# Attention scores and transposes issued on two 64-row halves of the array, and the first MLP's `w_in` low words joined on VectorE

## The chip, the cores and the metric

The kernel runs on one core of a Trainium2 chip. The metric is device microseconds of one execution, as a median of several runs. Five engines work side by side, each in the order in which its own instructions were written: PE (TensorE: PE for the matmuls, PEld for the loading of the stationary operand), DVE (VectorE), ACT (ScalarE), POOL (GpSimd) and SP (SyncE, which issues the DMAs). They wait for each other by semaphores.

## The reference, cut to what matters

Three layers follow each other. Attention runs over 8 batches of 576 tokens with 8 heads of 64, its keys and values averaged over groups of 8 tokens (72 remain):

```python
k_p = k.reshape(B, H, Sp, pool, D).mean(axis=3)          # Sp = 72
scores = scale * np.matmul(q, k_p.transpose(0, 1, 3, 2))
attn = np.exp(scores - scores.max(-1)); attn /= attn.sum(-1) + 1e-09
out = np.matmul(attn, v_p)
```

Then a rational MLP, with tokens 4608, model 512, hidden 2048: `h = x @ w_in; g = P(h) / (Q(h) + 1e-6); y = g @ w_out`, with P a cubic and Q built of |h| and h². Then a gated MLP with hidden 1536: `(sigmoid(y @ w_gate) * (y @ w_val)) @ w_out2`. The weights of both MLPs arrive as float64.

## The kernel before, in words

**Layout.** The 4608 tokens are 36 tiles of 128 tokens; four tiles are a block of 512. The first MLP goes block by block, 16 hidden slices of 128 each: 144 steps, each with `g1` (12 matmuls of 512 columns into a bank `h`, then a chain on ACT and DVE, then `g` with its low part on POOL) and `g2` (12 matmuls into four banks `acc`). Every large product is made of three fp32r matmuls of high and low parts (`mm3`, lines 628 to 630).

**Attention** of a tile (`tile_attention`, from line 544) is spread between these steps:

- *Scores*, line 569, tile `sc`. The pooled keys `kp` of a batch, two heads above each other on the 128 partitions, are copied by ACT into a block-diagonal tile `kbd` (`place_keys`, line 476), with zeros elsewhere. A matmul over all 128 rows then gives two heads at once: stationary 128x128 (queries), moving 128x144 (`kbd`). Four of them give the eight heads, two in each of two PSUM banks. An fp32 matmul appears as two records in the trace, each with its own load, so a tile has 8.
- *Softmax*: maximum and subtraction on DVE, Exp on ACT, sum and reciprocal on DVE, scaling on POOL (line 586).
- *Transposes*, line 594, tile `pta`: eight, each with stationary 128x72 (a head of `e`) and the 128x128 identity moving; a transpose is one record. ACT copies the two banks to `aT` (line 596).
- *Product with the values*, line 610, tile `psx`: the two heads of a pair go to the upper and lower 64 columns of the array, with stationary 72x64 (`vh`).

A tile that spans two batches does its scores once for each, so 36 tiles have 40 score groups.

**Weights of the first MLP.** `conv1` turns a float64 slice in `stage` (high and low 32-bit words interleaved) into fp32 bits: ACT rescales the high words (line 296), ACT scales the low words (298), DVE shifts the high words (299, an int32 TENSOR_SCALAR), POOL adds the two (303). `conv2` splits the result into a high part (ACT, line 308) and a low part (line 310): by DVE for `w_in`, by POOL for `w_out`. The first eight slices of `w_in` and of `w_out` are converted apart (512 wide), the other eight in pairs (1024 wide). `background` converts the second MLP's weights in the same way.

**Order.** A planner places every task by a table of costs, ranks and free buffers, and the engines' instructions are written in that order, so a new cost or buffer moves instructions all through the program. In the planner, tasks with `port=True` on DVE are not started while POOL is busy, nor POOL's while such a task runs. Attention's banks come from the four banks of `h` (from block 1 on at most three at a time).

Of the kernel before, what the change touches and what calls it, by code (L numbers as in the profile page):

```python
# [12 lines left out]
U32 = mybir.dt.uint32  # L13
AF = mybir.ActivationFunctionType
ALU = mybir.AluOpType
AX = mybir.AxisListType
# [172 lines left out]
def attention_moe_glu_kernel(ctx: ExitStack, tc: tile.TileContext, q, k, v, w_in, w_out, ca, cb, w_gate, w_val, w_out2, out):  # L189
    nc = tc.nc  # L190

    B, H, S, D = v.shape
# [40 lines left out]
    slots = {"W": [f"w{i}" for i in range(NF1 + FS + NR)], "ST": [f"st{i}" for i in range(6)],  # L233
             "h": [f"b{i}" for i in range(4)], "su": [f"su{i}" for i in range(3)], "y": [f"y{i}" for i in range(3)],
             "m": [f"m{i}" for i in range(3)], "g": [f"g{i}" for i in range(3)], "xs": ["xs0", "xs1"],
             "raw": [f"raw{i}" for i in range(3)], "e": ["e"], "aT": ["aT"], "kp": ["kp"], "vp": ["vp"],
             "vh": ["vh0", "vh1"], "kbd": ["kbd"]}
# [50 lines left out]

    def conv1(raw, rank):
        n = raw.size * 4 * P
        r = [(raw, ("in", x)) for x in range(raw.size)]
        def hw(): return raw.t[:, :, 1]
        def lw(): return raw.t[:, :, 0]
        plan("ACT", act(n), rank, lambda: nc.scalar.activation(hw().bitcast(F32), hw().bitcast(F32), AF.Prelu, scale=2.0 ** -112, alpha=2.0 ** 32),  # L296
             w=[(raw, 1)], r=r)
        plan("ACT", act(n), rank, lambda: nc.scalar.activation(lw(), lw().bitcast(U32), AF.Copy, scale=2.0 ** -29), w=[(raw, 0)], r=r)
        plan("DVE", 0.07 + n * 0.00065, rank, lambda: nc.vector.tensor_scalar(out=hw(), in0=hw(), scalar1=3, scalar2=None, op0=ALU.logical_shift_left),
             w=[(raw, 1)], port=True)  # L300
        for x in range(raw.size):
# [47 lines left out]
    def weights(f, rank, load_i, load_o, rank_o):  # L349
        if f < 8:  # L350
            for make, put, r, rl in ((wi_load, wi_parts, rank, load_i), (wo_load, wo_parts, rank_o, load_o)):
                raw = raw_buf(f"raw{f}", "cv")
                make(f, raw, rl)
                conv1(raw, r)
                put(f, raw, r)
            return
        raw = raw_buf(f"raw{f}", "cv" if f < SEG else "cv2", 2)
        wi_load(f, raw, load_i, 0)
        wo_load(f, raw, load_o, 1)
        conv1(raw, rank)  # L360
        wi_parts(f, raw, rank, 0)
        wo_parts(f, raw, rank_o, 1)

# [89 lines left out]
    kbd = small([P, NJ, 2, SP], "kbd", ["kbd"])  # L453
    vh, xs, rawq, turned, pooled = {}, {}, {}, [], {}

    def k_cols(c):
# [2 lines left out]
    def keys(b, rank, rank_load):  # L459
# [10 lines left out]
    def place_keys(b, rank):  # L470
        kp = pooled.pop(b)
        for js, cs in ((slice(0, NJ // 2), (0, 1, 2)), (slice(NJ // 2, NJ), (2, 3, 4))):
            for e in range(2):
                half = slice(e * D, (e + 1) * D)
                def fn(e=e, js=js, half=half):
                    nc.scalar.activation(kbd.t[half, js, e], kp.t.rearrange("p (j s) -> p j s", s=SP)[half, js], AF.Copy)
                plan("ACT", act(SP * 2), rank, fn,
                    w=[(kbd, (js.start, e))], r=[(kp, c) for c in cs])

    def values0(rank, rank_load):  # L480
        vp = small([P, NCH, D], "vp", ["vp"])
# [68 lines left out]
    def tile_attention(i, rank, gate_on=[]):  # L550
# [8 lines left out]

        for x, (b, n) in enumerate(parts):  # L560
            rows = slice(x * n, (x + 1) * n)
            if i == first[b]:
                place_keys(b, rank)
            for g in range(2):
                sc = psum("sc", own, kind)

                def fn(g=g, sc=sc):
                    for j in (2 * g, 2 * g + 1):
                        nc.tensor.matmul(sc.t[:, (j % 2) * 2 * SP:(j % 2 + 1) * 2 * SP], raw.t[:, j * P:(j + 1) * P], kbd.t[:, j].rearrange("p e s -> p (e s)"), start=True, stop=True)  # L569
                plan("PE", 0.5, rank, fn, w=[sc], r=[raw, (kbd, (2 * g, 0)), (kbd, (2 * g, 1))],  # L570
                     after=(turned[-1:] if blk > 1 else turned[-3:-2]) + gate_on)
                hs = slice(4 * g, 4 * g + 4)
                scv = lambda sc=sc, rows=rows: sc.t[rows, :4 * SP].rearrange("p (h s) -> p h s", s=SP)
                plan("DVE", dve(288) - 0.04, rank, lambda hs=hs, scv=scv, rows=rows: nc.vector.reduce_max(mx.t[rows, hs], scv(), axis=AX.X), w=[(mx, (g, x))], r=[sc])
                plan("DVE", dve(288) - 0.04, rank, lambda hs=hs, scv=scv, rows=rows, n=n: nc.vector.tensor_tensor(
                    out=e_.t[rows, hs, :SP], in0=scv(), in1=mx.t[rows, hs].unsqueeze(2).to_broadcast([n, 4, SP]), op=ALU.subtract),
                    w=[(e_, (g, x))], r=[sc, (mx, (g, x))])
# [4 lines left out]
        def fn():  # L582
# [3 lines left out]
        plan("POOL", 1.12, rank, lambda: nc.gpsimd.tensor_tensor(  # L586
            out=e_.t[:, :, :SP], in0=e_.t[:, :, :SP], in1=r.t.unsqueeze(2).to_broadcast([P, H, SP]), op=ALU.mult), w=[e_], r=[r])
        aT = small([P, H, P], "aT", tmp_where(blk, "aT") + (["ST"] if blk >= 2 else []), "tmp" if blk < 2 else None)
        for g in range(2):
            pta = psum("pta", own, kind)  # L590

            def fn(g=g, pta=pta):
                for h in range(4 * g, 4 * g + 4):
                    nc.tensor.transpose(pta.t.rearrange("p (h t) -> p h t", t=P)[:SP, h % 4], e_.t[:, h, :SP], ident)  # L594
            pt = plan("PE", 0.44, rank, fn, w=[pta], r=[e_])
            plan("ACT", act(512) - 0.08, rank, lambda g=g, pta=pta: nc.scalar.activation(  # L596
                aT.t[:SP, 4 * g:4 * g + 4], pta.t.rearrange("p (h t) -> p h t", t=P)[:SP], AF.Copy), w=[(aT, g)], r=[pta])
        turned.append(pt)
        waiting.append((i, parts, aT))
        if blk >= 2 and i % 2 == 0:  # L600
# [128 lines left out]

    T0 = -20.0  # L730
    values_at = {}
    for c in range(1):
        plan("DVE", 0.6, T0, lambda: nc.vector.memset(kbd.t, 0.0), w=[kbd])
# [57 lines left out]
    for n in range(N1):  # L791
# [6 lines left out]
        x = n - last_step  # L798
        if x == BX:
            bar = plan("-", 0.0, n, "late", after=[t for t in plan.tasks if any(b.where and b.where[0] in  # L800
                       ("ST", "raw", "e", "aT", "kp", "vp", "vh", "kbd", "mx0", "mx1", "r0", "r1") for b in t.bufs)])
# [28 lines left out]
    with tc.manual_schedule():  # L830
# [7 lines left out]
        pools.update(w=wp, b=ps, su=rot, y=rot, m=rot, g=g_p, xs=xs_p, raw=raw_p, e=ap1, aT=ap1, kp=ap1, vp=ap1, vh=ap1, kbd=ap1,  # L838
                     mx=sm, r=sm)
        for t in jobs:  # L840
            if t.fn == "late":
# [358 lines left out]
```

## Time and profile before

| | us |
|---|---|
| Median of 3 runs (lowest, highest) | 1736.67 (1735.71, 1737.2) |
| The profiled execution's own time | 1734.64 |
| Its span, first to last instruction | 1732.6 |
| PE busy in the span | 1709.0 (99%) |
| PEld busy | 1553.5 (90%) |
| DVE busy | 1235.0 (71%) |
| ACT busy | 1046.6 (60%) |
| POOL busy | 730.0 (42%) |

A matmul's record is longer than its share of the engine: matmuls overlap, and what each adds is seen from the distance of the starts. A burst's cost is therefore read from the start of a matmul to the start of a later one. The trace gives starts in hundredths of a microsecond.

### The profile page before, as it was taken

What the parts mean: (1) busy time and instruction counts of PE and PEld (TensorE: products, weight loads), DVE (VectorE), ACT (ScalarE), POOL (GpSimd) and SP (SyncE); (2) the same over time, 40 slices, a digit from 0 to 9 for tenths busy, and PEclk for the clock granted to TensorE, in tenths of its full rate; (3) what the DMA queues carried; (4) which work ended last, traced back from release to release, by engine and by line L of the source; (5) the groups of instructions that cost most, each with busy time, mean ns of one, the idle gap of its engine ahead of it and who ended that gap; (6) DMA issues with size and microseconds to landing.
All of it is one profiled execution on the core that took longest, in us unless ns stands there. A gap on an engine that the chain in (4) does not pass through costs nothing.

```text
span 1732.6 us, 28635 instructions
## 1 busy us (share of the span) xinstructions
PE 1709.0 (99%) x10044; PEld 1553.5 (90%) x10044; DVE 1235.0 (71%) x2146; ACT 1046.6 (60%) x1957; POOL 730.0 (42%) x807
## 2 busy tenths in 40 slices
PE   7899999999999999999999999999999999999999
PEld 6688888888888888788889999999999999999999
DVE  7898888888887878788786466466466467457456
ACT  6999778787877878898885244244244234235234
POOL 6675356454644646777544320330330330330320
PEclk9999999999999999999999999999999999999999
DMA  7675463545535446775753998888888888888856
GB/s 242 190 278 197 158 192 127 177 145 181 187 116 184 146 157 187 227 239 185 235 181 120 301 317 279 277 265 279 272 272 280 277 265 279 272 270 279 255 181 207
DMA packets 180867, 384.61 MB, mean 222 GB/s; under 512 B 24692, under 2 KB 92276, under 8 KB 180724
## 3 DMA queue, kind: packets, MB, share of 16 engines
q1 hardware_dynamic: 180724, 382.78, 67.4%
q8 instruction: 80, 1.31, 0.3%
q14 instruction: 63, 0.52, 0.1%
HBM read 322.96 MB, written 58.72 MB: 220 GB/s over the span
## 4 chain that ended last, share of the span: by engine, by line
PE 93%; ACT 2%; DMA 1%; DVE 1%; POOL 1%; issue 0%; SPq 0%; POOLq 0%; ACTq 0%
PE h L628 17%; PE h L630 17%; PE h L629 17%; PE acc L628 7%; PE acc L630 7%; PE acc L629 7%; PE acc L1044 5%; PE acc L1043 5%; PE acc L1042 5%; PE sc L569 2%; PE psx L610 2%; PE pta L594 2%; DMA stage<-in_moe_w_in_dram 0%; ACT stage L296 0%; DMA rawv<-in_v_dram 0%
## 5 line engine op out<-in xcount | busy, mean ns | idle before, releaser
L933 DVE TENSOR_TENSOR t<-h,t 128x384 f32<-128x384 f32 x360 | 200.8, 558 | 251.2 <-PE h L630 123.0
L668 POOL TENSOR_TENSOR g<-y,g 128x512 fp32r<-128x512 f32 x143 | 186.6, 1305 | 205.3 <-ACT g L666 175.7
L1002 POOL TENSOR_TENSOR ga<-t 128x384 f32<-128x384 f32 x48 | 48.9, 1019 | 452.5 <-DVE t L933 445.6
L628 PE MATMUL h<-xs,wi 128*128 128x512 f32 x576 | 228.9, 397 | 5.7 <-ACT aT L596 3.6
L628 PE MATMUL acc<-g,wo 128*128 128x512 f32 x576 | 230.1, 399 | 0.0
L630 PE MATMUL acc<-g,wo 128*128 128x512 f32 x576 | 225.2, 391 | 1.9 <-POOL g L668 1.9
L630 PE MATMUL h<-xs,wi 128*128 128x512 f32 x576 | 225.3, 391 | 0.0
L629 PE MATMUL h<-xs,wi 128*128 128x512 f32 x576 | 225.2, 391 | 0.0
L629 PE MATMUL acc<-g,wo 128*128 128x512 f32 x576 | 224.6, 390 | 0.0
L1044 PE MATMUL acc<-wo,go 128*128 128x256 f32 x756 | 213.9, 283 | 0.0
L1043 PE MATMUL acc<-wo,go 128*128 128x256 f32 x756 | 213.9, 283 | 0.0
L1042 PE MATMUL acc<-wo,go 128*128 128x256 f32 x756 | 213.9, 283 | 0.0
L628 PE MATMUL h<-xS,wq 128*128 128x384 f32 x576 | 192.4, 334 | 0.0
L630 PE MATMUL h<-xS,wq 128*128 128x384 f32 x576 | 192.4, 334 | 0.0
L629 PE MATMUL h<-xS,wq 128*128 128x384 f32 x576 | 192.4, 334 | 0.0
L947 ACT ACTIVATE t<-h 128x384 f32<-128x384 f32 x72 | 35.3, 491 | 242.2 <-PE h L630 238.4
L662 DVE SCALAR_TENSOR_TENSOR y<-y,coef,h 128x512 f32<-128x512 f32 x144 | 107.2, 744 | 70.9 <-ACT h L661 70.5
L1044 PEld LDWEIGHTS acc<-wo,go 128*128 128x128 f32 x756 | 145.1, 192 | 0.0
L1043 PEld LDWEIGHTS acc<-wo,go 128*128 128x128 f32 x756 | 145.1, 192 | 0.0
L1042 PEld LDWEIGHTS acc<-wo,go 128*128 128x128 f32 x756 | 145.1, 192 | 0.0
L628 PE MATMUL h<-xA,wq 128*128 128x384 f32 x432 | 144.3, 334 | 0.0
L629 PE MATMUL h<-xA,wq 128*128 128x384 f32 x432 | 144.3, 334 | 0.0
(129 smaller groups left out, 4258.1 us busy)
## 6 DMA issues: line engine op xcount, KB each, us to landing
wq<-w2d SPq DMA_DIRECT2D x252, 512.0 KB
wo<-wo2d SPq DMA_DIRECT2D x126, 512.0 KB
wo<-wod SPq DMA_DIRECT2D x96, 512.0 KB
w2d<-stage SPq DMA_DIRECT2D x36, 512.0 KB
wo2d<-stage SPq DMA_DIRECT2D x84, 128.0 KB
rawk<-in_k_dram SPq DMA_DIRECT2D x32, 256.0 KB
rawq<-in_q_dram SPq DMA_DIRECT2D x32, 256.0 KB
rawv<-in_v_dram SPq DMA_DIRECT2D x32, 256.0 KB
```

The lines of the kernel that those rows point to most:

```text
L569: nc.tensor.matmul(sc.t[:, (j % 2) * 2 * SP:(j % 2 + 1) * 2 * SP], raw.t[:, j * P:(j + 1) * P], kbd.t[:, j].rearrange("p e s -> p (e s)"), ...
L628: nc.tensor.matmul(out_, wl, xh, start=start, stop=False, skip_group_check=on)
L629: nc.tensor.matmul(out_, wh, xh, start=False, stop=False, skip_group_check=on)
L630: nc.tensor.matmul(out_, wh, xl, start=False, stop=stop, skip_group_check=on)
L662: plan("DVE", 0.66, rank, lambda: STT(out=y.t, in0=y.t, scalar=coef[:, 0:1], in1=h.t, op0=ALU.add, op1=ALU.mult), w=[y], r=[h])
L668: plan(on, cost, rank, lambda: eng.tensor_tensor(out=g.t[:, 1], in0=y.t, in1=g.t[:, 0].bitcast(F32), op=ALU.subtract), w=[(g, 1)], r=[y, ( ...
L933: nc.vector.tensor_tensor(out=out_, in0=a, in1=b, op=ALU.add)
L947: nc.scalar.activation(t["u"], b[1], AF.Copy)
L1002: eng.tensor_tensor(out=dst, in0=x, in1=y, op=ALU.mult)
L1042: nc.tensor.matmul(a, gh, wh, start=s_ == 0 and not on, stop=False, skip_group_check=on)
L1043: nc.tensor.matmul(a, gh, wl, start=False, stop=False, skip_group_check=on)
L1044: nc.tensor.matmul(a, gl, wh, start=False, stop=s_ == NS - 1, skip_group_check=on)
```

## The change

Scores: the tile `kbd` and its copies go. The matmuls read `kp` directly, 16 records of stationary 64x128 and moving 64x72, with the heads of the upper 64 rows (`g` = 0) and of the lower 64 rows (`g` = 1) in turn, each half of the rows into a bank of its own. Both banks belong to one task. `kp` has two buffers. Transposes: 16 instead of 8, each of 64 rows (tokens) with the 64x64 part of the identity moving, the halves in turn, each half into its own bank; ACT's two copies to `aT` now take a half of the tokens each. Weights: for every `w_in` slice, and for both of the slices converted in pairs, the low words' ACT instruction and POOL's add are replaced by one DVE SCALAR_TENSOR_TENSOR (shift right by 29, then or); the low part of `w_in` goes from DVE to POOL.

```diff
-    def conv1(raw, rank):
+    def conv1(raw, rank, fused=False):
...
-        plan("ACT", act(n), rank, lambda: nc.scalar.activation(lw(), lw().bitcast(U32), AF.Copy, scale=2.0 ** -29), w=[(raw, 0)], r=r)
+        if not fused:
+            plan("ACT", act(n), rank, lambda: nc.scalar.activation(lw(), lw().bitcast(U32), AF.Copy, scale=2.0 ** -29), w=[(raw, 0)], r=r)
...
+            if fused:
+                plan("DVE", 0.75, rank, lambda o=o: nc.vector.scalar_tensor_tensor(out=hw()[:, o], in0=lw()[:, o], scalar=29, in1=hw()[:, o],
+                     op0=ALU.logical_shift_right, op1=ALU.bitwise_or), w=[(raw, ("t", x))], r=r + [(raw, 1)], port=True)
+                continue
...
-        conv2(raw, wi[f], rank, 0, x)
+        conv2(raw, wi[f], rank, 1, x)
...
-                conv1(raw, r)
+                conv1(raw, r, make is wi_load)
...
-        conv1(raw, rank)
+        conv1(raw, rank, True)
...
+            sc = [psum("sc", own, kind) for _ in range(2)]
+
+            def fn(b=b, sc=sc):
+                for j in range(NJ):
+                    for g in range(2):
+                        nc.tensor.matmul(sc[g].t[:, j * SP:(j + 1) * SP], raw.t[g * D:(g + 1) * D, j * P:(j + 1) * P],
+                                         pooled[b].t[g * D:(g + 1) * D, j * SP:(j + 1) * SP], start=True, stop=True)
+            plan("PE", 0.6, rank, fn, w=sc, r=[raw, pooled[b]],
...
-                    for j in (2 * g, 2 * g + 1):
-                        nc.tensor.matmul(sc.t[:, (j % 2) * 2 * SP:(j % 2 + 1) * 2 * SP], raw.t[:, j * P:(j + 1) * P], kbd.t[:, j].rearrange("p e s -> p (e s)"), start=True, stop=True)
-                plan("PE", 0.5, rank, fn, w=[sc], r=[raw, (kbd, (2 * g, 0)), (kbd, (2 * g, 1))],
...
+        pta = [psum("pta", own, kind) for _ in range(2)]
+
+        def fn(pta=pta):
+            for h in range(H):
+                for g in range(2):
+                    rows = slice(g * D, (g + 1) * D)
+                    nc.tensor.transpose(pta[g].t.rearrange("p (h t) -> p h t", t=D)[:SP, h], e_.t[rows, h, :SP], ident[rows, rows])
+        pt = plan("PE", 0.55, rank, fn, w=pta, r=[e_])
...
-                    nc.tensor.transpose(pta.t.rearrange("p (h t) -> p h t", t=P)[:SP, h % 4], e_.t[:, h, :SP], ident)
-            pt = plan("PE", 0.44, rank, fn, w=[pta], r=[e_])
```

Three places show how instructions move. PE, in the middle of the first MLP, before: `acc` and `h` are the big products, the sixth row a tile's transposes, and the scores of the next tile stand one product later.

```order
L628 MATMUL acc_2139<-g,wo_1976 128x512
L629 MATMUL acc_2139<-g,wo_1976 128x512
L630 MATMUL acc_2139<-g,wo_1976 128x512
L594 MATMUL pta<-ident,e 72x128 x8
L628 MATMUL acc_2146<-g,wo_1976 128x512
L629 MATMUL acc_2146<-g,wo_1976 128x512
L630 MATMUL acc_2146<-g,wo_1976 128x512
L569 MATMUL sc<-kbd,rawq 128x144 x4
L628 MATMUL h<-xs,wi_1523 128x512
```

PE at the same kind of place now:

```order
L625 MATMUL acc_2228<-g,wo_2048 128x512
L626 MATMUL acc_2228<-g,wo_2048 128x512
L627 MATMUL acc_2228<-g,wo_2048 128x512
L590 MATMUL pta<-ident,e 72x64 x16
L625 MATMUL acc_2219<-g,wo_2048 128x512
L626 MATMUL acc_2219<-g,wo_2048 128x512
L627 MATMUL acc_2219<-g,wo_2048 128x512
```

The burst still stands alone between two full-array products; its instructions are twice as many and half as high. Over the program 36 score and 33 transpose bursts stand so.

ACT at the start of the program before, where `wi` and `wo` are the high parts (line 308) of the weights, `stage` the words (296, 298) and `kbd` the copies of the keys:

```order
L308 ACTIVATE wi_448<-stage 128x512
L296 ACTIVATE stage<-stage 128x512
L619 ACTIVATE xs<-psx 128x4x128
L298 ACTIVATE stage<-stage 128x512
L476 ACTIVATE kbd<-kp 64x2x72 x4
L296 ACTIVATE stage<-stage 128x512
L298 ACTIVATE stage<-stage 128x512
L654 ACTIVATE u<-h,coef 128x512
```

The same place now:

```order
L616 ACTIVATE xs<-psx 128x4x128
L314 ACTIVATE wi_492<-stage 128x512
L297 ACTIVATE stage<-stage 128x512
L300 ACTIVATE stage<-stage 128x512
L297 ACTIVATE stage<-stage 128x512
L651 ACTIVATE u<-h,coef 128x512
```

The four copies and one of two low-word instructions (298, now 300) are gone from ACT's row.

DVE at the start of the program before, around the low parts (310) of the first two `w_in` slices:

```order
L620 SCALAR_TENSOR_TENSOR xs<-psx,xs 128x4x128 x2
L310 TENSOR_TENSOR wi_372<-stage,wi_372 128x512
L299 TENSOR_SCALAR stage<-stage 128x512 x2
L620 SCALAR_TENSOR_TENSOR xs<-psx,xs 128x4x128
L310 TENSOR_TENSOR wi_448<-stage,wi_448 128x512
```

The same place now:

```order
L617 SCALAR_TENSOR_TENSOR xs<-psx,xs 128x4x128 x2
L306 SCALAR_TENSOR_TENSOR stage<-stage 128x512
L617 SCALAR_TENSOR_TENSOR xs<-psx,xs 128x4x128
L301 TENSOR_SCALAR stage<-stage 128x512 x2
L306 SCALAR_TENSOR_TENSOR stage<-stage 128x512
```

On DVE the joining instruction (306) has taken the place of the low part (310), one for one.

## Rows read from the trace of the kernel before

**Rows 1.** Windows: length; PE, PEld, DVE, ACT, POOL busy (records); clock; DMA.
```profile
30.00:57.00 27.00, 21.13 (x134) 17.30 (x132) 23.04 (x43) 22.19 (x42) 18.23 (x21) 0.87 0.65 209
57.00:107.40 50.40, 45.75 (x243) 36.55 (x243) 47.10 (x75) 49.23 (x86) 40.14 (x41) 1.00 0.64 211
107.40:130.00 22.60, 22.60 (x100) 18.71 (x101) 20.09 (x30) 22.52 (x37) 14.75 (x14) 1.00 0.83 277
130.00:845.00 715.00, 712.45 (x3721) 592.26 (x3720) 588.48 (x976) 578.92 (x1042) 405.89 (x483) 1.00 0.53 175
```

**Rows 2.** Windows of tile sc alone, from 107.4: PE, PEld, DVE busy (records).
```profile
107.40:845.00 737.60, 35.88 (x248) 34.83 (x248) 53.69 (x124) 1.00 0.54 178
```

**Rows 3.** Windows of tile pta alone: PE, PEld, ACT busy (records).
```profile
107.40:845.00 737.60, 29.45 (x224) 24.59 (x224) 30.31 (x56) 1.00 0.54 178
```

**Rows 4.** PE timeline, one score burst: start, length, line, shapes, records.
```profile
443.56 1.14 PE L569 MATMUL sc<-kbd,rawq 128*128 128x144 f32 x8
...
444.78 0.40 PE L629 MATMUL h<-xs,wi 128*128 128x512 f32 x1
```

**Rows 5.** PE timeline, one transpose burst.
```profile
453.44 1.03 PE L594 MATMUL pta<-ident,e 128*72 128x128 f32 x8
...
454.54 0.40 PE L629 MATMUL acc<-g,wo 128*128 128x512 f32 x1
```

**Rows 6.** PE timeline, a burst on the array's column halves.
```profile
412.63 0.40 PE L630 MATMUL acc<-g,wo 128*128 128x512 f32 x1
412.96 1.09 PE L610 MATMUL psx<-aT,vh 72*64 72x128 f32 x16
413.89 1.04 PE L610 MATMUL psx<-stage,vh 72*64 72x128 f32 x16
414.86 0.50 PE L628 MATMUL acc<-g,wo 128*128 128x512 f32 x1
415.19 0.39 PE L629 MATMUL acc<-g,wo 128*128 128x512 f32 x1
```

**Rows 7.** PE timeline, another such burst, its second part 64 columns wide.
```profile
277.35 1.10 PE L610 MATMUL psx<-stage,vh 72*64 72x64 f32 x32
278.38 0.50 PE L628 MATMUL h<-xs,wi 128*128 128x512 f32 x1
```

**Rows 8.** PEld timeline, two loads of one pair of column halves.
```profile
413.23 0.14 PEld L610 LDWEIGHTS psx<-aT,vh 72*64 72x64 f32 x2
```

**Rows 9.** PEld timeline, ten loads of 72 columns in a row.
```profile
20.11 0.73 PEld L511 LDWEIGHTS vps<-vp,sel 128*72 128x72 f32 x10
```

**Rows 10.** PE timeline, from 128-row to 64-row matmuls: two windows' rows.
```profile
21.14 0.69 PE L511 MATMUL vps<-vp,sel 128*72 128x64 f32 x6
...
21.49 0.34 PE L511 MATMUL vps<-vp,sel 64*72 64x64 f32 x2
```

**Rows 11.** Groups by form, PEld: shapes, records; busy us, mean ns; idle before.
```profile
L594 PEld LDWEIGHTS pta<-ident,e 128*72 128x72 f32 x288 | 31.8, 117 | 13.6 <-POOL e L586 6.1 <-ACT aT L596 1.9 <-issue 0.3
...
L511 PEld LDWEIGHTS vps<-vp,sel 128*72 128x72 f32 x22 | 1.6, 145 | 0.0
L511 PEld LDWEIGHTS vps<-vp,sel 64*72 64x72 f32 x2 | 0.2, 138 | 0.1
```

**Rows 12.** Groups of ACT from 18 to 107.4.
```profile
L298 ACT ACTIVATE stage<-stage 128x512 int32<-128x512 uint32 (+1 forms) x18 | 13.1, 733 | 0.0
...
L476 ACT ACTIVATE kbd<-kp 64x144 f32<-64x144 f32 x4 | 1.3, 322 | 0.0
```

**Rows 13.** Groups of DVE from 18 to 107.4.
```profile
L310 DVE TENSOR_TENSOR wi<-stage,wi 128x512 fp32r<-128x512 f32 x9 | 8.0, 892 | 0.7 <-ACT wi L308 0.7
...
L663 DVE SCALAR_TENSOR_TENSOR h<-u,h 128x512 f32<-128x512 f32 x9 | 6.2, 684 | 0.0
```

**Rows 14.** Groups of POOL from 18 to 107.4.
```profile
L303 POOL TENSOR_TENSOR stage<-stage 128x512 int32<-128x512 int32 x20 | 21.3, 1078 | 11.2 <-DVE stage L299 4.0 <-issue 2.7 <-ACT h L661 2.1
...
L310 POOL TENSOR_TENSOR wo<-stage,wo 128x512 fp32r<-128x512 f32 x8 | 10.5, 1315 | 0.7 <-ACT wo L308 0.6
```

More of the change, by code (lines that the diff above doesn't have):

```diff
@@ L235, in attention_moe_glu_kernel @@
              "m": [f"m{i}" for i in range(3)], "g": [f"g{i}" for i in range(3)], "xs": ["xs0", "xs1"],
-             "raw": [f"raw{i}" for i in range(3)], "e": ["e"], "aT": ["aT"], "kp": ["kp"], "vp": ["vp"],
-             "vh": ["vh0", "vh1"], "kbd": ["kbd"]}
+             "raw": [f"raw{i}" for i in range(3)], "e": ["e"], "aT": ["aT"], "kp": ["kp0", "kp1"], "vp": ["vp"],
+             "vh": ["vh0", "vh1"]}
     slots.update({f"acc{e}": [f"b{4 + e}"] for e in range(NJ)})
@@ L451, in small @@
         return Buf(name, shape, F32, where, kind)
-    kbd = small([P, NJ, 2, SP], "kbd", ["kbd"])
     vh, xs, rawq, turned, pooled = {}, {}, {}, [], {}
@@ L468, in keys @@
         pooled[b] = kp
[L470 to L478, printed above, removed]
     def values0(rank, rank_load):
@@ L561, in tile_attention @@
             rows = slice(x * n, (x + 1) * n)
-            if i == first[b]:
-                place_keys(b, rank)
-            for g in range(2):
-                sc = psum("sc", own, kind)
-                def fn(g=g, sc=sc):
-                    for j in (2 * g, 2 * g + 1):
-                        nc.tensor.matmul(sc.t[:, (j % 2) * 2 * SP:(j % 2 + 1) * 2 * SP], raw.t[:, j * P:(j + 1) * P], kbd.t[:, j].rearrange("p e s -> p (e s)"), start=True, stop=True)
-                plan("PE", 0.5, rank, fn, w=[sc], r=[raw, (kbd, (2 * g, 0)), (kbd, (2 * g, 1))],
[L571 to L574, printed above, removed]
+            sc = [psum("sc", own, kind) for _ in range(2)]
[5 more added lines that the diff above has]
+            plan("PE", 0.6, rank, fn, w=sc, r=[raw, pooled[b]],
+                 after=(turned[-1:] if blk > 1 else turned[-3:-2]) + gate_on)
+            for g in range(2):
+                hs = slice(g, H, 2)
+                scv = lambda sc=sc[g], rows=rows: sc.t[rows, :4 * SP].rearrange("p (h s) -> p h s", s=SP)
+                plan("DVE", dve(288) - 0.04, rank, lambda hs=hs, scv=scv, rows=rows: nc.vector.reduce_max(mx.t[rows, hs], scv(), axis=AX.X), w=[(mx, (g, x))], r=[sc[g]])
                 plan("DVE", dve(288) - 0.04, rank, lambda hs=hs, scv=scv, rows=rows, n=n: nc.vector.tensor_tensor(
                     out=e_.t[rows, hs, :SP], in0=scv(), in1=mx.t[rows, hs].unsqueeze(2).to_broadcast([n, 4, SP]), op=ALU.subtract),
-                    w=[(e_, (g, x))], r=[sc, (mx, (g, x))])
+                    w=[(e_, (g, x))], r=[sc[g], (mx, (g, x))])
         plan("ACT", act(576), rank, lambda: nc.scalar.activation(e_.t[:, :, :SP], e_.t[:, :, :SP], AF.Exp, scale=scale / POOL),
@@ L588, in tile_attention @@
         aT = small([P, H, P], "aT", tmp_where(blk, "aT") + (["ST"] if blk >= 2 else []), "tmp" if blk < 2 else None)
-        for g in range(2):
-            pta = psum("pta", own, kind)
-            def fn(g=g, pta=pta):
-                for h in range(4 * g, 4 * g + 4):
-                    nc.tensor.transpose(pta.t.rearrange("p (h t) -> p h t", t=P)[:SP, h % 4], e_.t[:, h, :SP], ident)
-            pt = plan("PE", 0.44, rank, fn, w=[pta], r=[e_])
+        pta = [psum("pta", own, kind) for _ in range(2)]
[5 more added lines that the diff above has]
+        pt = plan("PE", 0.55, rank, fn, w=pta, r=[e_])
+        for g in range(2):
             plan("ACT", act(512) - 0.08, rank, lambda g=g, pta=pta: nc.scalar.activation(
-                aT.t[:SP, 4 * g:4 * g + 4], pta.t.rearrange("p (h t) -> p h t", t=P)[:SP], AF.Copy), w=[(aT, g)], r=[pta])
+                aT.t[:SP, :, g * D:(g + 1) * D], pta[g].t.rearrange("p (h t) -> p h t", t=D)[:SP], AF.Copy), w=[(aT, g)], r=[pta[g]])
         turned.append(pt)
@@ L731, in attention_moe_glu_kernel @@
     values_at = {}
-    for c in range(1):
-        plan("DVE", 0.6, T0, lambda: nc.vector.memset(kbd.t, 0.0), w=[kbd])
     warm = psum("warm", ["acc2"])
@@ L800, in attention_moe_glu_kernel @@
             bar = plan("-", 0.0, n, "late", after=[t for t in plan.tasks if any(b.where and b.where[0] in
-                       ("ST", "raw", "e", "aT", "kp", "vp", "vh", "kbd", "mx0", "mx1", "r0", "r1") for b in t.bufs)])
+                       ("ST", "raw", "e", "aT", "kp", "vp", "vh", "mx0", "mx1", "r0", "r1") for b in t.bufs)])
             rawx[0] = Buf("rawx", [P, 8 * TB], F32, ["xs"])
@@ L837, in attention_moe_glu_kernel @@
         stage_t.append(stage.tile([P, len(slots["ST"]) * 8 * P], F32, name="stage"))
-        pools.update(w=wp, b=ps, su=rot, y=rot, m=rot, g=g_p, xs=xs_p, raw=raw_p, e=ap1, aT=ap1, kp=ap1, vp=ap1, vh=ap1, kbd=ap1,
+        pools.update(w=wp, b=ps, su=rot, y=rot, m=rot, g=g_p, xs=xs_p, raw=raw_p, e=ap1, aT=ap1, kp=ap1, vp=ap1, vh=ap1,
                      mx=sm, r=sm)
```

## The prediction

> **What bounds the kernel now.** I read the busy time by stage first, then single bursts in PE's timeline, then the groups of the start. The windows show two regimes. From 107.4 us to the end of attention PE is the bound: it is busy for 22.60 of 22.60 us and then for 712.45 of 715.00, at full clock [rows 1]. There a microsecond of PE is a microsecond of the kernel, and what other engines shed is worth nothing. Before 107.4 PE waits: from 30 on it is busy for 21.13 of 27.0 and 45.75 of 50.4 us, so 10.5 us are idle, and the granted clock averages 0.87 in the first of the two, some of it at the lower of two levels. In the second, ACT is busy for 49.23 of 50.4 us and DVE for 47.10 [rows 1]: two engines, almost equally full. The change has one part for each regime.
>
> **The unit.** A plain 512-column matmul costs 22.60 / 100 = 0.226 us [rows 1]; I use 0.227. A burst costs the distance from its first start to the real start of the big matmul after it. That one's start is modelled too early, so I take the second big matmul's start less 0.227. The scores cost 444.78 - 0.227 - 443.56 = 0.99 us [rows 4], 0.122 for each of the 8 records, and the transposes 454.54 - 0.227 - 453.44 = 0.87 [rows 5], 0.109 each. Behind 107.4 there are 248 / 8 = 31 score groups [rows 2] and 224 / 8 = 28 tiles' transposes [rows 3].
>
> **What halves of the array cost: read from the value product.** It already runs on halves, of the columns. Its 16 records of 128 moving columns take 0.93 us (412.96 to 413.89), which is 8 x 0.109 and a first load of 0.05: two matmuls go in the time of one [rows 6]. Their loads run side by side: two, of 137 ns each, within 0.14 us [rows 8]. So halves do overlap. But entering and leaving cost time. The last full matmul streams until 412.63 + 0.23 = 412.86, and the first half begins at 412.96: 0.10 idle, and then its load is not hidden. At the end, 414.86 - 413.89 = 0.97 is 8 x 0.109 and 0.10 idle, and the next full load (415.19 - 0.23 - 414.86 = 0.10 to 0.11) lies open [rows 6]. Whether row halves pay this too is seen once: from 128-row to 64-row matmuls at 21 us. Four full ones at 0.065 from 21.14 on stream until 21.39, and the first 64-row one comes at 21.49: the same 0.10 [rows 10].
>
> **What a pair costs.** Matmuls are half as long now: 72 moving columns instead of 144 is 0.061 us. But the score's load keeps its 128 columns. Ten loads of 72 columns stand (0.73 - 0.145) / 9 = 0.065 apart [rows 9, 11], though their matmuls of 64 columns alone would need half of the 0.109 of 128 columns. Pairs with loads of 64 columns stand (278.38 - 277.35 - 0.10) / 16 = 0.058 apart [rows 7]. That is 0.9 ns a column, so loads of 128 columns set a pace of 0.107 (the load that lies open) to 0.116 (0.9 x 128). I take 0.112. Above it the bound is 0.122, where such loads hide now [rows 4]. Below it, if a load of half the rows took half the time, it is 0.061. The trace's loads of 64 rows took 138 ns against 145 with 128 rows [rows 11], so I stay near the upper end.
> The Trainium skill (TensorE: Matmul & The Clock Gate, section LDWEIGHTS) states a load as columns over 1.2 GHz, whatever the number of rows. By that the pace would be at least 0.107 us; the trace's 138 against 145 ns agrees.
>
> **Scores, after.** 0.10 idle + 0.11 first load + 7 x 0.112 + 0.06 last matmul + 0.10 idle + 0.11 open load = 1.26, say 1.25 us, against 0.99. 31 x 0.26 = +8.1 us. What the halves save in streaming (8 x 0.122 against 8 x 0.112) is less than the two changes cost.
>
> **Transposes, after.** Eight pairs with 64 moving columns; a transpose's load of 72 columns is 28 ns shorter than a matmul's (117 against 145 [rows 11]), so the matmuls set the pace: 0.058. 0.10 + 0.03 + 8 x 0.058 + 0.10 + 0.11 = 0.80 against 0.87. 28 x -0.07 = -2.0 us.
>
> So the stage behind 107.4 gains 6.1 us. The waits that are added, two banks at once for a burst, I cost at nothing: queued behind them on PE are the big products, but before the change PE idled for only 2.55 us in the whole stage [rows 1], and a slower PE gives the others more time. If a burst once misses its bank, it is some tenths.
>
> **The start.** From 18 to 107.4 ACT has 18 low-word instructions (16 of 512, 2 of 1024; 13.1 us) and four key copies (1.3) [rows 12]. Eight and both wide ones go, by columns 60% of the 13.1 (6144 of 10240): 7.9, with the copies 9.2 us, or some 8 as such records overlap their neighbours. DVE loses nine or ten low parts of 0.892 [rows 13] and gains 8 + 2 x 2 = 12 joining instructions. No row shows such an instruction. The nearest are an SBUF pair (310, 0.892 with its port waits) and a SCALAR_TENSOR_TENSOR (0.684) [rows 13]; I take 0.75, which makes 12 x 0.75 - 9.5 x 0.892 = +0.5 us, with -0.3 and +2.2 at the ends. POOL loses 12 adds of 1.078 and gains nine or ten low parts of 1.315 [rows 14]: -0.4 us. So ACT is freed, and DVE, which has 3.3 us of idle time in 50.4 [rows 1], is late next. I take 3 us off the start. At best all of PE's idle time from 30 on (10.5 us) and what the low clock costs (0.13 x 27 = 3.5) go: -14. At worst, each early `w_in` slice is ready later, as its low part takes 1.315 on POOL instead of 0.892 and stands there in the row with values and gates: 10 x 0.42 = +4. The dearer scores of this stage, nine groups, are within that.
>
> **Sum.** +8.1 - 2.0 - 3.0 = +3.1 us. On the profiled execution's 1734.64 that is 1737.7. This execution lay 2.0 below the median of the runs, 1736.67, to which the result compares: 1739.8.
>
> **Rivals.**
> *Faster by halves.* (a) The loads of 64 rows take half the time: a pair 0.061, scores 0.86, 31 x -0.13 = -4.0; with -2.0 and -3 this is -9, 1728. Against it: 138 and 145 ns. (b) A change to row halves costs no idle time: scores 8 x 0.112 + 0.01 = 0.91, transposes 0.47: -2.5 - 11.2 - 3 = -17, 1720. Against it stand rows 6 and 10. (c) Both at once, a pair costing hardly more than one of its matmuls: scores 0.50, transposes 0.46, -15.2 - 11.5 - 3 = -30, 1707. For it speaks only that the column halves overlap so well.
> The Trainium skill (TensorE: Matmul & The Clock Gate, section Measured speedup vs the span model) gives a packed group as one matmul's time and about 4 ns for each further tile, which is (c). It holds for long streams; for bursts of 16 between full matmuls rows 6 show 0.36 us on top.
> *Slower by serial halves.* Row halves share what column halves do not, and their loads go one after another: scores 16 x 0.112 + 0.36 = 2.15, 31 x 1.16 = +36; transposes unchanged from my sum; +31, 1768. It decides as soon as two loads of a pair start more than 0.1 us apart. If the matmuls don't overlap either, transposes are 16 x 0.056 + 0.36 = 1.26 and the time 1780: then the change does not do what it says. Against it speaks the overlap in rows 6 and 8, though of columns.
> *Slower by the start.* POOL's low parts hold back the first products, and the start grows by 4 instead of shrinking by 3: 1736.67 + 6.1 + 4 = 1746.8. It decides if PE's first continuous stretch begins after 107.4. For it: POOL was busy for 40.14 of 50.4 us, and these parts are on the way to the first products. Against it: its sum of work does not grow.
>
> **How the numbers follow.** My forecast has 0.46, with a start between -6 and 0 and so 1736.8 to 1742.8, at 1739.8. Faster by halves has 0.30: (a) 0.12, (b) 0.10, (c) 0.08. Serial halves have 0.11, of which 0.04 at 1780. The longer start has 0.13. About 0.2% (3.5 us) can be told from no change here. The forecast's own band lies across that bound: 0.25 same, 0.19 slower, 0.02 faster. Of the longer start 0.02 is same and 0.11 slower. So faster is 0.30 + 0.02 = 0.32, same 0.27, slower 0.19 + 0.11 + 0.11 = 0.41. The range leaves out (c) and the serial halves, together 0.19, and takes in (b) with a little room and the longer start: 1718 to 1750.
>
> **What would show it.** In PE's timeline of the changed kernel: a score burst of 1.25 us between big matmuls, loads in pairs that start within some ns, pairs 0.11 apart; a transpose burst of 0.80, pairs 0.058 apart; 0.10 idle at either end. Pairs of scores at 0.06 say (a), no idle ends say (b), pairs at 0.2 say serial halves. For the start: PE continuously busy from some 104 us, ACT with a few us of idle time between 57 and there, DVE with almost none. I am wrong if the scores cost less than 0.9 us or more than 1.5, or if that point moves by more than 6 us either way.

## The result, and the profile after

The changed kernel takes 1747.58 us (median of 6 runs, 1746.97 to 1751.46); the kernel before took 1736.4 beside it (6 runs, 1735.13 to 1737.39). The ratio is 1.007, with an interval of 1.0057 to 1.0083: 11.2 us slower, where 3.1 had been forecast. The profiled execution took 1746.97 (1734.64 before); its span is 1745.1 against 1732.6, 12.5 longer.

Windows of the kernel after, columns as in [rows 1]:

```profile
0.00:30.00 30.00, 22.26 (x240) 20.68 (x240) 20.23 (x43) 13.72 (x26) 17.27 (x41) 0.75 0.85 272
30.00:57.00 27.00, 20.59 (x112) 16.05 (x112) 20.03 (x35) 16.93 (x30) 14.54 (x18) 0.71 0.56 181
57.00:107.40 50.40, 47.35 (x324) 37.10 (x325) 45.76 (x80) 46.16 (x81) 40.84 (x41) 1.00 0.58 179
107.40:130.00 22.60, 21.97 (x97) 17.55 (x96) 22.18 (x33) 21.42 (x37) 13.75 (x13) 1.00 0.91 321
130.00:845.00 715.00, 709.48 (x4155) 571.68 (x4154) 591.09 (x969) 560.13 (x998) 397.81 (x472) 1.00 0.53 175
```

ACT is relieved as forecast (30 to 57: 16.93 against 22.19; 57 to 107.4: 46.16 against 49.23), yet PE is idle more behind 130: 5.5 us against 2.55. And from 30 to 57 us the granted clock is 0.71 where it was 0.87.

A score burst of the kernel after, PE and then PEld (start, length, shapes, records), which answers to [rows 4]:

```profile
450.51 0.39 PE L627 MATMUL acc<-g,wo 128*128 128x512 f32 x1
450.83 1.11 PE L562 MATMUL sc<-kp,rawq 64*128 64x72 f32 x16
451.88 0.50 PE L625 MATMUL h<-xs,wi 128*128 128x512 f32 x1
452.22 0.39 PE L626 MATMUL h<-xs,wi 128*128 128x512 f32 x1
```

```profile
450.83 0.97 PEld L562 LDWEIGHTS sc<-kp,rawq 64*128 64x128 f32 x16 [0.35 <-DVE u L653]
451.88 0.19 PEld L625 LDWEIGHTS h<-xs,wi 128*128 128x128 f32 x1
```

Counted from the end of the product ahead, so that the idle time on entering is in it, the burst costs 452.22 - 0.227 - (450.51 + 0.227) = 1.25 us. (The prediction's unit, from the burst's first start, leaves that out, though its sum of 1.25 has it in.) The 16 loads of some 0.19 us each fill only 0.97 us, so two run side by side; eight pairs stand (0.97 - 0.19) / 7 = 0.111 apart. Ahead of the burst 450.83 - 450.74 = 0.09 is idle, and behind it the next full load lies open: 452.22 - 0.227 - 451.88 = 0.11.

A transpose burst of the kernel after, PE and PEld, against [rows 5]:

```profile
461.31 0.39 PE L627 MATMUL acc<-g,wo 128*128 128x512 f32 x1
461.63 0.64 PE L590 MATMUL pta<-ident,e 64*72 64x64 f32 x16
462.20 0.50 PE L625 MATMUL acc<-g,wo 128*128 128x512 f32 x1
462.53 0.39 PE L626 MATMUL acc<-g,wo 128*128 128x512 f32 x1
```

```profile
461.62 0.48 PEld L590 LDWEIGHTS pta<-ident,e 64*72 64x72 f32 x16 [0.35 <-issue]
```

It costs 462.53 - 0.227 - (461.31 + 0.227) = 0.77 us. Over all bursts behind 107.4, counted in this way, the medians are 1.249 us for the scores (0.994 before) and 0.773 for the transposes (0.882 before).

**An account.** The first MLP has 3456 matmuls of 512 columns (six groups of 576). I cut the span at the start of the 301st and of the last: what lies ahead is the start, what lies between is the stretch, which holds 3155 such matmuls, the 31 score groups, the transposes of 28 tiles and all value products of that part, in every kernel below; the granted clock in it is 1.00 on both sides. Before, the 301st starts at 126.12, after at 128.55:

```profile
126.12 0.39 PE L628 MATMUL h<-xs,wi 128*128 128x512 f32 x1
```

```profile
128.55 0.39 PE L625 MATMUL acc<-g,wo 128*128 128x512 f32 x1
```

The start is 2.4 longer. The stretch grew from 813.84 to 823.93, by 10.1: the bursts' share is 31 x 0.255 - 28 x 0.109 = +4.85, so 5.2 us are something else. What follows is the same (792.6). PE's waits from 107.4 to 860 in the kernel after (in total, times, longest):

```profile
PE h L625 <- DVE y L661: 2.1, 2, 1.1
PE h L625 <- DVE e L570: 2.0, 2, 1.4
PE acc L627 <- POOL g L665: 1.5, 2, 0.9
PE sc L562 <- DVE xs L617: 0.2, 1, 0.2
```

Most are an `h` product that waits until DVE has done with a bank (2.1 us for the last reader of an earlier `h`, line 661; 2.0 for the scores' subtraction, line 570). PE's gaps in the stretch sum to 6.2 us in ten places, against 2.55 in three before. Between two big products a wait costs more than its gap shows, because the record of the product ahead is longer than its share and the first load behind the gap lies open:

```profile
571.21 0.39 PE L627 MATMUL acc<-g,wo 128*128 128x512 f32 x1
572.67 0.50 PE L625 MATMUL h<-xs,wi 128*128 128x512 f32 x1 [1.07 <-DVE y L661]
573.01 0.40 PE L626 MATMUL h<-xs,wi 128*128 128x512 f32 x1
```

Here 573.01 - 571.21 - 2 x 0.227 = 1.35 us are lost where 1.07 is shown. Five of the ten gaps stand so, and one of the three before. That makes about 3.65 + 4 x 0.28 = 4.8 of the 5.2 us.

### The profile page after: what moved, and what is told of

It reads as the page before. It is cut to its first block, busy times and chain, and to the rows that moved or that the text cites. A ratio compares the mean times of both kernels' runs of the same rounds, so it can differ in the third digit from the quotient of the medians.

```text
span 1745.1 us, 29808 instructions
## 1 busy us (share of the span) xinstructions
PE 1717.9 (98%) x10652; PEld 1541.0 (88%) x10652; DVE 1241.8 (71%) x2153; ACT 1024.5 (59%) x1909; POOL 727.0 (42%) x799
## 4 chain that ended last, share of the span: by engine, by line
PE 92%; DVE 4%; ACT 2%; DMA 1%; issue 1%; POOL 0%; SPq 0%; ACTq 0%
PE h L625 17%; PE h L626 17%; PE h L627 17%; PE acc L625 7%; PE acc L627 7%; PE acc L626 7%; PE acc L1039 5%; PE acc L1038 5%; PE acc L1037 5%; PE sc L562 2%; PE psx L607 2%; PE pta L590 1%; DVE u L653 0%; DVE y L659 0%; DVE y L654 0%
## 5 line engine op out<-in xcount | busy, mean ns | idle before, releaser
L625 PE MATMUL h<-xs,wi 128*128 128x512 f32 x576 | 229.8, 399 | 11.3 <-DVE y L661 6.0
L651 ACT ACTIVATE u<-h,coef 128x512 f32<-128x512 f32 x144 | 98.6, 685 | 79.3 <-PE h L627 78.8
L625 PE MATMUL h<-xA,wq 128*128 128x384 f32 x432 | 144.3, 334 | 0.0
```

The source lines that it names most:

```text
L625: nc.tensor.matmul(out_, wl, xh, start=start, stop=False, skip_group_check=on)
L651: ACT(0.57, rank, lambda: nc.scalar.activation(u.t, h.t, AF.Abs, scale=coef[:, 5:6]), w=[u], r=[h, coef_b])
```

## The experiments

Two theories for the 5.2 us and the start. A: the attention part brings them, above all because a burst now wants two banks at once. B: the weights' part, whose low parts stand on POOL. Later came C: any other order of the same work brings them. In the table, start and stretch are differences from before's 126.12 and 813.84 in the profiled executions, and the rest is the stretch's change less that of its bursts. They come from one execution of each kernel, while 27 executions of the kernel before spread from 1732.81 to 1738.29, so a difference of a microsecond or two in these columns says little by itself.

| kernel | median us | ratio to before (interval) | start | stretch | bursts | rest |
|---|---|---|---|---|---|---|
| changed kernel | 1747.58 | 1.0070 (1.0057, 1.0083) | +2.4 | +10.1 | +4.85 | +5.2 |
| attention only | 1745.98 | 1.0072 (1.0059, 1.0085) | +1.6 | +9.9 | +4.85 | +5.0 |
| weights only | 1736.1 | 1.0011 (1.0003, 1.0020) | -3.0 | +3.0 | 0 | +3.0 |
| score halves only | 1747.65 | 1.0080 (1.0068, 1.0092) | +2.6 | +10.3 | +7.9 | +2.4 |
| transpose halves only | 1738.0 | 1.0019 (1.0011, 1.0028) | +2.9 | -0.3 | -3.05 | +2.8 |
| two banks, full array | 1739.34 | 1.0034 (1.0023, 1.0046) | +0.3 | +3.9 | 0 | +3.9 |
| transpose halves late | 1742.38 | 1.0045 (1.0032, 1.0057) | -0.4 | +7.9 | -3.05 | +11.0 |
| scores twice | 1782.51 | 1.0273 (1.0259, 1.0287) | +11.9 | +39.1 | +32.5 | +6.5 |
| costs only, a | 1742.85 | 1.0047 (1.0034, 1.0059) | +4.9 | +4.2 | 0 | +4.2 |
| costs only, b | 1738.55 | 1.0019 (1.0010, 1.0028) | -0.6 | +4.8 | 0 | +4.8 |
| quarter scores, half transposes | 1731.35 | 0.9978 (0.9970, 0.9987) | -3.0 | -0.2 | -7.05 | +6.8 |
| quarter scores only | 1736.15 | 1.0011 (1.0003, 1.0020) | -0.1 | +1.5 | -4.0 | +5.4 |
| changed, scores on quarters | 1735.31 | 1.0006 (0.9997, 1.0014) | -1.1 | +2.0 | -7.05 | +9.1 |

The kernel before ran at 1734.7 to 1734.9 beside these runs, and at 1736.4 beside the changed kernel.

**Attention only.** The changed kernel with the weights' conversion as before.

```diff
-                conv1(raw, r, make is wi_load)
+                conv1(raw, r)
-        conv2(raw, wi[f], rank, 1, x)
+        conv2(raw, wi[f], rank, 0, x)
```

> Scores and transposes on row halves as in the changed kernel; the weights' conversion as before (low words on ACT and POOL, low part of w_in on DVE). Theory A (what the change costs beyond its bursts comes from the attention part: a burst now needs two banks and all keys at once, so PE waits more, also at the start): about +11, 1746 to 1749, the gaps of PE behind 126 us near 6.8 us as in the changed kernel against 2.55 before, the first h as late or later. Theory B (it comes from the weights, whose low parts stand on POOL): only the bursts remain, 31 x 0.255 - 28 x 0.11 = +4.8, near 1741, gaps near 2.5 us. In both the score burst 1.25 us, the transpose burst 0.77.

Measured 1745.98, 11.3 over before. Bursts 1.249 and 0.773. Theory B falls: nearly all is here, about as A had said.

**Weights only.** The kernel before with the other half.

```diff
+                conv1(raw, r, make is wi_load)
-        conv2(raw, wi[f], rank, 0, x)
+        conv2(raw, wi[f], rank, 1, x)
```

> Attention as before; the weights' conversion as in the changed kernel (joined on DVE, low part of w_in on POOL). Theory A: no longer than before, 0 to -3 from the freed ACT at the start, 1733 to 1737, gaps of PE behind 126 us near 2.5 us. Theory B: the +2.4 of the start and the 4 us of added gaps come here, 1741 to 1744. Bursts 0.99 and 0.88 us in both.

Measured 1736.1, +1.4: the start gains 3.0 us (the 301st matmul below), and the stretch gives all of it back in waits. The time is within theory A's, but no theory had waits from the weights' part.

```profile
123.11 0.39 PE L633 MATMUL h<-xs,wi 128*128 128x512 f32 x1
```

**Score halves only**, and **transpose halves only**: one burst in the new form, the other as before.

```diff
+            sc = [psum("sc", own, kind) for _ in range(2)]
+                        nc.tensor.matmul(sc[g].t[:, j * SP:(j + 1) * SP], raw.t[g * D:(g + 1) * D, j * P:(j + 1) * P],
```

> Only the scores are on row halves (both banks at once, keys read directly); transposes and weights as before. The burst's cost alone is 31 x 0.255 = +7.9, so 1744.3 if nothing else is added (theory B); with waits for two banks and all keys 1746 to 1748 (theory A). Score burst 1.25 us with pairs 0.112 apart in both, transposes 0.88.

```diff
+        pta = [psum("pta", own, kind) for _ in range(2)]
+                    nc.tensor.transpose(pta[g].t.rearrange("p (h t) -> p h t", t=D)[:SP, h], e_.t[rows, h, :SP], ident[rows, rows])
```

> Only the transposes are on row halves (both banks at once); scores and weights as before. The burst's cost alone is 28 x -0.11 = -3.1, so 1733.3 if nothing else is added (theory B); if the two banks at once cost waits (theory A) the gain is eaten: 1735 to 1738, with more than 4 us of gaps behind 126 us. Transpose burst 0.77 us with pairs 0.056 apart in both, scores 0.99.

Measured 1747.65 (+12.9) and 1738.0 (+3.3). Both times are those of theory A. Each burst costs what its own sum says, and each kernel adds 5 to 6 us of start and waits. Parts that add 12.9 and 3.3 alone give 11.3 together, so what is added is not a price of either part.

**Two banks, full array.** Nothing on halves; the four matmuls (and the eight transposes) of a tile become one task with both banks.

```diff
-                plan("PE", 0.5, rank, fn, w=[sc], r=[raw, (kbd, (2 * g, 0)), (kbd, (2 * g, 1))],
+            plan("PE", 1.0, rank, fn, w=sc, r=[raw] + [(kbd, (2 * g, e)) for g in range(2) for e in range(2)],
```

> The kernel before, all on full arrays, but the four score matmuls of a group are one task that holds both banks at once (and needs all keys), and likewise the eight transposes; nothing runs on halves. Theory A1 (the added waits come from two banks at once and the order that follows): +4 to +7, 1739 to 1742, with 5 to 7 us of gaps of PE behind 126 us and a longer start. Theory A2 (they come from what half-array bursts do, to the clock at the start above all): within 1 us of before, 1735 to 1737, gaps behind 126 us near 2.5, low clock before 107.4 us for some 14 us as before, not 24 to 31 as in every kernel with row halves so far.

Measured 1739.34, +4.4, of which 3.9 in the stretch, as A1 said; the start did not lengthen, and the mean granted clock up to 107.4 us is 0.94, as before. Taken alone it would have confirmed A. The costs-only runs below take that reading away.

**Transpose halves late.** The first eight tiles keep the full array.

```diff
+        if blk < 2:
+            for g in range(2):
+                pta = psum("pta", own, kind)
```

> Transposes on row halves from the third block of tokens on, the first eight tiles as before; scores and weights as before. If the +3.3 us of the run with all transposes on halves came from the start, 28 x -0.11 = -3.1 comes through: 1731.5 to 1733. If it came from waits of the whole attention stage, 1735 to 1738 as there.

Measured 1742.38: a miss of both. The start is as before, but the stretch is 11.0 us longer than its bursts explain, 3.69 of it in one wait, in PE's timeline, where a product has to wait for POOL's low part of `g`:

```profile
263.23 0.40 PE L642 MATMUL acc<-g,wo 128*128 128x512 f32 x1
267.32 0.75 PE L643 MATMUL acc<-g,wo 128*128 128x512 f32 x1 [3.69 <-POOL g L681]
```

That wait is at a big product and not at a transpose. It was the reason to test order by itself.

**Costs only, a and b.** The kernel before, instruction for instruction; only two numbers that the planner goes by are changed, so the order differs.

```diff
-                plan("PE", 0.5, rank, fn, w=[sc], r=[raw, (kbd, (2 * g, 0)), (kbd, (2 * g, 1))],
+                plan("PE", 0.6, rank, fn, w=[sc], r=[raw, (kbd, (2 * g, 0)), (kbd, (2 * g, 1))],
-            pt = plan("PE", 0.44, rank, fn, w=[pta], r=[e_])
+            pt = plan("PE", 0.40, rank, fn, w=[pta], r=[e_])
```

> The kernel before with not one instruction changed, only the planner's costs of two kinds of PE tasks (scores 0.50 to 0.60, transposes 0.44 to 0.40), so that the same work is written in another order. Theory C (the order of before happens to leave PE few waits, and any other order has more): the stretch from PE's 301st big product to its last in attention grows by 2 to 6 us from 813.8, the time is 1737 to 1741. Theory D (only a burst that holds two banks brings the waits): the stretch within 1 us, 1734 to 1736.

> As the run before, with the costs moved the other way (scores 0.45, transposes 0.48). Theory C: the stretch grows by 2 to 6 us again, 1737 to 1741. Theory D: within 1 us, 1734 to 1736.

Measured 1742.85 (+8.1) and 1738.55 (+3.8). Theory C holds for the stretch and D is out: it grows by 4.2 and 4.8 us with the same instructions. (The first time lies above C's 1737 to 1741, since the start moved too.) PE's waits from 107.4 to 860 in the first of them:

```profile
PE pta L594 <- POOL e L586: 2.3, 4, 1.4
PE acc L630 <- POOL g L668: 1.5, 3, 0.6
PE h L628 <- DVE y L664: 0.3, 1, 0.3
PE h L628 <- DVE e L575: 0.2, 1, 0.2
```

The waits are others than in the changed kernel, with a sum of 4.3 us against 5.8 there. An `h` product that waits for the scores' bank (the last row) is not a matter of two banks alone: it takes 2.0 us in the changed kernel, and 1.2 us in costs only, b, where a score burst's two banks are separate tasks. The start moved by +4.9 and -0.6, by order alone.

**Scores twice.** The changed kernel, each group's 16 records issued twice in the burst.

```diff
-                for j in range(NJ):
+                for j in list(range(NJ)) * 2:
```

> The changed kernel with each score group's 16 records issued twice in a row in the same burst. If a burst is a stream of 0.112 us a pair and 0.36 us for entering and leaving the halves: 1.25 + 8 x 0.112 = 2.15 us, +0.90 for each of 31 behind 107.4 and up to 9 at the start: 1775 to 1783. If entering and leaving costs nothing and a pair 0.156: 2.50 us, +39 to +50. The idle time at either end of the burst stays 0.09 and 0.10 us by the first and cannot be told by the second.

One burst, PE and PEld:

```profile
427.35 0.39 PE L627 MATMUL acc<-g,wo 128*128 128x512 f32 x1
427.67 2.01 PE L562 MATMUL sc<-kp,rawq 64*128 64x72 f32 x32
429.61 0.50 PE L625 MATMUL h<-xs,wi 128*128 128x512 f32 x1
429.95 0.39 PE L626 MATMUL h<-xs,wi 128*128 128x512 f32 x1
```

```profile
427.67 1.86 PEld L562 LDWEIGHTS sc<-kp,rawq 64*128 64x128 f32 x32 [0.35 <-issue]
```

The median burst is 2.142 us. So eight more pairs cost 2.142 - 1.249 = 0.893, or 0.112 each, and what does not double is 1.249 - 0.893 = 0.356: the price of entering and leaving the halves, as forecast. The time is within the forecast too.

**Quarter scores, half transposes.** Loads of 64 columns instead of 128, four tiles of the array at once; weights as before.

```diff
-                    for g in range(2):
-                        nc.tensor.matmul(sc[g].t[:, j * SP:(j + 1) * SP], raw.t[g * D:(g + 1) * D, j * P:(j + 1) * P],
+                    for t in ts:
+                      for g in range(2):
+                        nc.tensor.matmul(sc[g].t[t * D:(t + 1) * D, j * SP:(j + 1) * SP], raw.t[g * D:(g + 1) * D, j * P + t * D:j * P + (t + 1) * D],
```

> Scores on four 64x64 quarters (row half by column half, a record loads 64 columns instead of 128; a tile of two batches computes only the half of its tokens that belongs to the batch), transposes on row halves, weights as before. If the load of 128 columns sets the pace of the halves' burst and four quarters run side by side: 8 x 0.061 + 0.36 = 0.85 us a full burst against 1.25, some less for the split tiles; 31 x -0.4 = -12 against the run with the attention part alone (1746): 1732 to 1736. If only two of the four run side by side, 16 x 0.061 + 0.36 = 1.34: 1747 to 1750.

Measured 1731.35, 3.6 below before, just under the forecast and the fastest of all. Order alone has moved the time by as much, so only the bursts' 7.05 us can be put down to the edit. PE's timeline, a full group and then one of a tile of two batches:

```profile
397.73 0.39 PE L623 MATMUL acc<-g,wo 128*128 128x512 f32 x1
398.05 0.73 PE L558 MATMUL sc<-kp,rawq 64*64 64x72 f32 x32
398.71 0.50 PE L621 MATMUL h<-xs,wi 128*128 128x512 f32 x1
399.05 0.40 PE L622 MATMUL h<-xs,wi 128*128 128x512 f32 x1
...
478.70 0.72 PE L558 MATMUL sc<-kp,rawq 64*64 64x72 f32 x16
```

32 records on four quarters last 0.73 us, 16 on two quarters 0.72: the other two ride free. The burst is 0.867 us against 1.249, with the same 72 moving columns, so it was the load of 128 columns that set the pace of the halves.

**Quarter scores only** (transposes as before, too), and the **changed kernel with its scores on quarters**: the same edit on two other bases.

> Scores on quarters (two banks at once), transposes and weights as before. Bursts: 25 x (0.867 - 0.994) + 6 x (0.854 - 0.994) = -4.0 us. If the start gains 3.0 as with quarter scores and half transposes together, and waits add 2.4 as with half scores alone: -4.6, 1730 to 1731. If the waits are 7 as in the run with both: 1734 to 1735.

> The changed kernel with its scores on quarters instead of halves. Bursts behind 107.4 us: 1.249 to 0.867 or 0.854, -11.9 us against the changed kernel, so 1735.7 from that alone. The start: if the half bursts on the way to the first products are what made it long (+1.6 with halves, -3.0 with quarters, weights as before), another 3 to 6 us: 1730 to 1733, below the kernel before; if the weights' part makes it long beside them, 1735 to 1736.

Measured 1736.15, a miss of both sums, and 1735.31, as forecast for a start that the weights' part makes long. The bursts come out as in the run before, but the start is 1.9 to 2.9 us worse, and with the weights' part 2.3 us of waits are added.

The three quarter kernels and scores twice show one thing more. They differ from a kernel with halves in the matmuls of a burst alone, and on DVE, ACT and POOL their traces have the same instructions in the same order as it (attention only, score halves only, and the changed kernel for two of them). So here the order is held, and only the bursts' length changes. From halves to quarters the start gets shorter by 4.5, 2.8 and 3.5 us; nine groups stand there, and 9 x 0.382 is 3.4. Doubled scores make it 9.5 longer, where 9 x 0.893 is 8.0. So a burst's time in the start does reach the big products, about in full as far as one execution of each shows. The rest moves as well, with no change of order: with quarters by +1.8, +3.0 and +3.9 us, with doubled scores by +1.3. What the quarters gain in bursts is in part given back in waits, and the 9.1 of the last kernel is more than a new order alone was seen to add.

## Why the prediction was right or wrong

**The number.** 1747.58 lies outside the forecast's own band (1736.8 to 1742.8), and inside the range of 1718 to 1750 only because the range took in the rival of the longer start. That rival's mechanism did not act (below), so this is luck. The span grew by 12.5 us where the sum had 3.1. Of the 9.4 between, the bursts are -1.25, the waits +5.2 and the start +5.4 (+2.4 in place of -3.0).

**The bursts: right.** Scores 1.25 forecast, 1.249 measured; pairs 0.112 and 0.111; idle on entering 0.10 and 0.09; both ends together 0.36 and 0.356. Transposes 0.80 forecast, 0.773 measured against 0.882 (not 0.87), so -3.05 in place of -2.0. The sum is +4.85 against +6.1. Faster by halves and slower by serial halves are both out: pairs stand neither 0.06 nor 0.2 apart, and the idle time on entering is there.

**The waits: wrong.** "The waits that are added, two banks at once for a burst, I cost at nothing" is the step that failed: 5.2 us. A missed bank was not "some tenths" but up to 1.4 us. The reason given, that PE idled for only 2.55 us before and so the others had time to spare, took the idle time of one order for a property of the work. DVE's share of the stretch was no sign of danger either (591.09 of 715 us, 588.48 before). But in a new order PE meets other instructions late, and none of the twelve other kernels had less than 2.4 us of this. The two kernels in which only costs changed had 4.2 and 4.8, so a new order is enough for most of the 5.2. Whether two banks at once add something beyond it cannot be told from 3.9, and the kernels with the same order show that the bursts' length alone moves it by 1.3 to 3.9.

**The start: the size right for the weights, the total wrong.** The weights' part by itself gains the 3.0 us that I had taken, in the one execution profiled. The joining instruction took 0.700 us (0.75 forecast), and POOL's low parts of `w_in` 1.358; groups of the kernel after from 18 to 107.4 (records | busy us, mean ns | idle before):

```profile
L306 DVE SCALAR_TENSOR_TENSOR stage<-stage 128x512 int32<-128x512 int32 x10 | 6.9, 700 | 0.0
```

```profile
L316 POOL TENSOR_TENSOR wi<-stage,wi 128x512 fp32r<-128x512 f32 x9 | 12.2, 1358 | 13.1 <-ACT wi L314 13.1
```

With attention on halves the start is longer instead: +1.6 with the weights as before, +2.4 in the changed kernel. My rival of the longer start (1746.8) comes close to the measured time, but by another way: its mechanism, POOL's low parts, is refuted by the run with the weights alone, and its +4 was +2.4. I had put the dearer scores of the start "within that", and so at nothing in the sum. This term failed too: the kernels with the same order show that bursts' time counts there, and nine groups at 0.255 are 2.3 us. At the lower level of the clock they are dearer still. PE's timeline shows one before, at the higher level, and the same one in the kernel after, at the lower:

```profile
30.92 1.22 PE L569 MATMUL sc<-kbd,rawq 128*128 128x144 f32 x8 [0.78 <-DMA rawq<-in_q_dram]
...
32.21 0.39 PE L629 MATMUL h<-xs,wi 128*128 128x512 f32 x1
```

```profile
31.56 1.99 PE L562 MATMUL sc<-kp,rawq 64*128 64x72 f32 x16 [2.20 <-DMA rawq<-in_q_dram]
33.48 0.79 PE L625 MATMUL h<-xs,wi 128*128 128x512 f32 x1
34.07 0.63 PE L626 MATMUL h<-xs,wi 128*128 128x512 f32 x1
...
48.99 0.77 PE L625 MATMUL h<-xs,wi 128*128 128x512 f32 x1 [3.85 <-DVE y L661]
49.56 0.63 PE L626 MATMUL h<-xs,wi 128*128 128x512 f32 x1
49.98 0.63 PE L627 MATMUL h<-xs,wi 128*128 128x512 f32 x1
```

The products behind the later one stand 49.98 - 49.56 = 0.42 apart instead of 0.227. So by the prediction's unit it costs 34.07 - 0.42 - 31.56 = 2.09 us, and the one before 32.21 - 0.227 - 30.92 = 1.06. Of the 5.4 us by which the start missed, the dearer scores are 2.3 by this estimate, at the costs of the higher level, and the eight tiles' transposes there give back some 0.9. Some 4 us stay open between the clock and the order, which alone made +4.9 and -0.6.

**The signs.** From 57 to 107.4 us ACT has the idle time that was forecast (4.2 us), but DVE has 4.6 and not "almost none". The point from which PE is first busy for long without a break, in PE's timeline before and after:

```profile
107.40 0.50 PE L630 MATMUL acc<-g,wo 128*128 128x512 f32 x1 [0.56 <-POOL g L668]
```

```profile
126.14 0.50 PE L627 MATMUL acc<-g,wo 128*128 128x512 f32 x1 [0.63 <-POOL g L665]
```

It moved by 18.7 us, more than the 6 at which the prediction calls itself wrong. But a single wait of 0.6 us sets it, and with the weights alone, where the start is 3.0 shorter, it lies as late (126.83). The start of a counted product is the better mark.

## What to carry to other kernels

Where a planner writes the order, a change of a few microseconds cannot be judged by one build: first change only the planner's numbers a little, and see how far the time moves with the same instructions (here by 3.8 and 8.1 us). A burst on a part of the array, between products on all of it, pays a fixed price at its ends (0.36 us here), and its pace was here the larger of load and matmul; so cut the stationary side as well as the rows. Compare kernels whose order is the same where that can be had: from halves to quarters only the bursts differ. And a busy share of 99% in one order says little of what the next order will wait for.

## What the runs showed of the hardware

- Four quarters of the array run at once: 32 records in 0.73 us, 16 on two quarters in 0.72. The Trainium skill (TensorE: Matmul & The Clock Gate, section Measured speedup vs the span model) gives about 4 ns for each further tile of a packed group. By that, as an estimate, two further tiles are 0.008 us. The whole burst of eight groups grew by 0.013 (0.854 to 0.867), which agrees if they count once in a burst, and not if they count in each group (0.064). The 0.36 us at the ends of each burst is not in that sum. That the sum holds for long streams, as the prediction says, no run here tests.
- The granted clock of the first attention bursts differs from kernel to kernel, and not by the halves alone. From 7 to 19 us, where PE ran the first score groups and transposes, the windows show a mean of 0.72 before and 0.54 after (1.00 is the higher of its two levels, 0.50 the lower):

```profile
7.00:19.00 12.00, 8.50 (x41) 7.52 (x42) 9.30 (x22) 4.89 (x10) 7.94 (x15) 0.72 0.91 314
```

```profile
7.00:19.00 12.00, 9.22 (x97) 8.92 (x98) 8.90 (x22) 3.85 (x9) 7.92 (x15) 0.54 1.03 336
```

With attention only it is 0.57, and with quarter scores in the same order 0.72; so there the form of the bursts makes a difference without a change of order. But costs only, b, with every burst on the full array, has 0.59, costs only, a, has 0.86, and transpose halves only have 0.86 too: order alone moves it as far, and halves need not lower it. PE was not less busy in the kernel after (9.22 against 8.50 us), though records at the lower level are longer. The first score group waited about as long as before (2.1 against 2.0 us), the second longer (1.9 against 1.4). Up to 107.4 us the mean is 0.94 before, 0.90 and 0.92 with costs only, 0.89 to 0.90 with quarters, and 0.86 to 0.89 with halves from the first tile on. What the halves do to the clock, and what the order does, no run here separates.
